# Threshold attention feeding a SoLU block: weights assembled by integer operations, early reciprocals on VectorE, one early block transfer on ScalarE's queue

## The chip, the cores and the metric

The kernel runs on one core of one Trainium2 chip. The metric is the device time of one execution in microseconds (us). All times here are in us unless marked otherwise. The engines are named as the profile names them: PE is TensorE (PEld its weight loads), DVE VectorE, ACT ScalarE, POOL GpSimd, SP SyncE; SPq and ACTq are the sequencers of SP and ACT while they issue a DMA.

## What is computed

Attention with a threshold on 8 batches of 8 heads, 576 tokens and 64 values a head, and then a feed-forward block over 4608 tokens:

```python
scores = scale * np.matmul(q, k.transpose(0, 1, 3, 2))
thresh = np.max(scores, axis=-1, keepdims=True) - tau
scores = np.where(scores >= thresh, scores, -1000000000.0)
scores = scores - np.max(scores, axis=-1, keepdims=True)
attn = np.exp(scores)
attn = attn / (np.sum(attn, axis=-1, keepdims=True) + 1e-09)
attn_out = np.matmul(attn, v)
...
x = attn_out.transpose(0, 2, 1, 3).reshape(B * S, H * D)
h = x @ w_in
solu = h * softmax(h)
ln = (solu - mean) / np.sqrt(var + 1e-06) * g_ln
return ln @ w_out
```

`q`, `k`, `v` are float32. `w_in` (512 x 1024) and `w_out` (1024 x 512) are float64; the launch hands them over as int64 words, and the kernel itself makes float32 of them from the two 32-bit halves.

## The kernel before, in words

The attention is cut into 144 *slots* of two heads by 128 rows of scores (18 a batch: kinds 0 and 1 are the 512 first columns of tokens, kind 2 the leftover 64). Two slots of the same heads are a *unit*. A Python loop walks over *rounds*, one new slot a round, and writes out by hand the order in which every engine gets its instructions; each engine then works through its own list in that order. In one round `rnd`:

- PE: `scores` (L480) of slot `rnd` into two PSUM tiles `s0`, `s1`. There is one buffer of each, so the next slot's scores wait until the ramps have read both.
- DVE: `maxes` (L502), for each of the two tiles the row extreme less the threshold, into `nth`.
- ACT: `ramp` (L517) of tile 0, then of tile 1, then `exps` (L526) of both, with the row sums into `sm`. Copies that prepare later heads (`keeps`, L382 to L427) stand between the two ramps in rounds with such items, and `whole_pair` copies after the exps in rounds 0, 2 and 4.
- POOL: `normalise` of slot `rnd - 1`: add 1e-9 (L533), power of -1 (L534), two products of the weights with the inverse (L536).
- DVE: `blocks` of slot `rnd - 1`: two transposes (L548) into `T`. After the second slot of a unit SP sends `T` to `wT` in three transfers (L557 for the middle partitions, L559 twice for the outer ones; kind 2 has four, L564).
- PE: `attend_steps` (L590), the product of `wT` with `v`, for a unit whose second slot is three rounds old (four in the first ones); ACT then copies it to `xh` (L622).
- PE: one of four steps of a feed-forward piece of 128 tokens: two h steps (L645, L655) and two o steps (L760), each half a piece's work, in successive rounds.

In rounds 0 to 15 one of 16 pieces of the weights (128 x 512 each; eight of `w_in` to `w1`, eight of `w_out` to `w2`) is made as well. `weight_load` (L275) brings the raw words, four rounds ahead. `weight_a` takes the exponent out of the high word on DVE (L286), turns it into a float scale on ACT (L291), and takes the mantissa bits (L292). `weight_b`, a round later, adds the low word (L306) and joins the sign to the scale (L309), both on DVE. `weight_c`, again a round later, multiplies the two on POOL (L319). For `w_out`, `weight_gain` first multiplies the scale by `g_ln` on ACT (L325), and `weight_d` sends the finished piece to its partner partitions on SP (L332, two transfers). `w2_done` is set with the last of these, in round 16; no o step is placed before that.

Two more facts of the order matter. POOL's `mark` (L109) waits for an h step of PE. Rounds past 16 in which no feed-forward step is under way are *loose*: there the maxima copy the scores out of PSUM, so that the ramps don't hold it.

## Time and profile before

| | |
|---|---|
| median of 3 runs | 866.67 us (865.36, 866.67, 873.14) |
| span of the profiled execution, first to last instruction | 865.3 us |
| instructions | 36120 |
| PE busy | 820.6 us, 95% |
| DVE busy | 682.6 us, 79% |
| ACT busy | 574.2 us, 66% |
| POOL busy | 500.2 us, 58% |
| DMA, queue of SP | 164.25 MB, 76.2% of 16 engines' span |
| DMA, queue of ACT | 2.00 MB, 0.7% |

The profiled execution has no time of its own in the list of runs; its span is what is known of it, and it lies 0.1 us under the fastest run. A busy share is a mean over the whole span: the first 100 us and the rest have different limits, so the prediction reads stretches of it. In the answers "x2" counts instructions, an arrow in brackets names what ended an idle time, and a line number is that of the kernel before.

### The profile page before, as it was taken

How to read it: one execution, taken by the hardware profiler on the slowest of the kernel's cores; microseconds unless marked ns; L12 is line 12 of the kernel's file. 1: busy time of each engine (PE TensorE's matmuls, PEld its weight loads, DVE VectorE, ACT ScalarE, POOL GpSimd, SP SyncE). 2: the span in 40 equal slices, each digit the busy share in tenths (PEclk: the TensorE clock that was granted, in tenths of full speed). 3: DMA queues.
4: the chain of work that ended last, by engine and by line, in shares of the span. 5: the costliest groups of instructions: out<-in, count | busy, mean ns of one | idle time of the engine just before them, and what ended most of it. 6: DMA issues, size and time to landing. Idle time of an engine off the chain costs nothing.

```text
span 865.3 us, 36120 instructions
## 1 busy us (share of the span) xinstructions
PE 820.6 (95%) x15361; PEld 633.6 (73%) x15361; DVE 682.6 (79%) x1248; ACT 574.2 (66%) x1153; POOL 500.2 (58%) x938
## 2 busy tenths in 40 slices
PE   5667999899999999999999999999999999999997
PEld 3444667677688887777777776777799998887655
DVE  4999778878788888888788887888888888787361
ACT  5887767767767767677677776777677776775121
POOL 2888656556656656565656655565666655555120
PEclk9788899999999999999999999999999999999999
DMA  8999787988878788988878877887788877655212
GB/s 256 273 261 238 192 190 176 229 237 203 222 188 232 200 191 197 225 221 191 212 190 223 204 188 186 220 221 203 190 224 229 205 180 189 154 142 139 69 38 62
DMA packets 83712, 168.54 MB, mean 195 GB/s; under 512 B 15448, under 2 KB 45152, under 8 KB 83552
## 3 DMA queue, kind: packets, MB, share of 16 engines
q1 hardware_dynamic: 82416, 164.25, 76.2%
q8 instruction: 120, 1.97, 1.0%
q10 hardware_dynamic: 1136, 2.00, 0.7%
q14 instruction: 40, 0.33, 0.1%
HBM read 46.14 MB, written 9.44 MB: 64 GB/s over the span
## 4 chain that ended last, share of the span: by engine, by line
PE 81%; DMA 7%; ACT 4%; DVE 2%; SPq 2%; issue 2%; POOL 1%; ACTq 0%; DVEq 0%
PE o_ps L760 26%; PE h_ps L655 22%; PE s_ps L480 15%; PE pv L590 15%; PE h_ps L645 3%; DMA wT<-T 3%; ACT w L517 1%; ACT w L526 1%; DMA ends<-in_q_dram 1%; DVE w L502 1%; DMA w<-w 1%; DMA qT<-flip 1%; DMA k<-in_k_dram 1%; DVE T L548 1%; POOL w L536 1%
## 5 line engine op out<-in xcount | busy, mean ns | idle before, releaser
L760 PE MATMUL o_ps<-w,uT 64*64 64x256 f32 x4608 | 274.3, 376 | 2.4 <-DMA w<-w 1.3
L502 DVE CUSTOM_DVE_ANT_0 w<-s_ps,tau_t 128x576 f32<-128x576 f32 x280 | 200.3, 753 | 87.5 <-PE s_ps L480 57.5
L517 ACT ACTIVATE w<-s_ps,nth 128x576 f32<-128x576 f32 x280 | 197.0, 739 | 104.9 <-DVE nth L502 94.1
L760 PEld LDWEIGHTS o_ps<-w,uT 64*64 64x64 f32 x4608 | 215.3, 133 | 62.8 <-ACT xh L622 11.0
L536 POOL TENSOR_SCALAR w<-w,sm 128x576 f32<-128x576 f32 x288 | 222.2, 784 | 14.3
L655 PE MATMUL h_ps<-w,xh 64*64 64x512 f32 x1856 | 225.3, 592 | 1.1 <-issue 1.1
L548 DVE STREAM_TRANSPOSE T<-w 128x576 f32<-128x576 f32 x288 | 207.6, 755 | 19.8 <-POOL w L536 19.4
L526 ACT ACTIVATE w<-w,ntau 128x576 f32<-128x576 f32 x288 | 219.6, 767 | 0.0
L590 PEld LDWEIGHTS pv<-wT,v 64*64 64x64 f32 x5760 | 179.0, 136 | 32.4 <-issue 8.5
L480 PE MATMUL s_ps<-kT,qT 64*64 64x64 f32 (+1 forms) x2048 | 183.2, 422 | 14.0 <-ACT w L517 12.1
L590 PE MATMUL pv<-wT,v 64*64 64x128 f32 (+1 forms) x5760 | 177.7, 264 | 7.4 <-DMA wT<-T 4.7
L655 PEld LDWEIGHTS h_ps<-w,xh 64*64 64x64 f32 x1856 | 134.8, 134 | 65.4 <-issue 15.6
L533 POOL TENSOR_SCALAR sm<-sm 128x2 f32<-128x2 f32 x144 | 36.5, 253 | 202.0 <-ACT w L526 198.9
L534 POOL TENSOR_TENSOR sm<-sm,mone 128x2 f32<-128x2 f32 x144 | 109.0, 757 | 12.0
L480 PEld LDWEIGHTS s_ps<-kT,qT 64*64 64x64 f32 x2048 | 78.3, 139 | 23.4 <-ACT w L517 17.3
L622 ACT COPY xh<-pv 128x256 f32<-128x256 f32 x64 | 25.2, 394 | 81.3 <-PE pv L590 81.3
L721 ACT ACTIVATE V<-u,nb,rs 128x1024 f32<-128x1024 f32 x36 | 44.7, 1241 | 38.8 <-POOL nb L711 31.8
L747 DVE STREAM_TRANSPOSE uT<-V 128x1024 f32<-128x1024 f32 x36 | 44.2, 1226 | 16.9 <-DMA V<-u 16.8
L526 ACT ACTIVATION_READ_ACCUMULATOR w<-w,ntau 128x1 f32 x288 | 55.5, 193 | 0.0
L685 DVE TENSOR_TENSOR u<-h_ps,u 128x1024 f32<-128x1024 f32 x36 | 42.8, 1189 | 9.8 <-ACT u L679 9.8
L726 DVE TENSOR_SCALAR u<-u,rs,nb 128x1024 f32<-128x1024 f32 x36 | 35.0, 973 | 17.8 <-ACT V L721 17.7
L670 DVE TENSOR_REDUCE hm<-h_ps 128x1 f32<-128x1024 f32 x36 | 42.9, 1193 | 5.4 <-PE h_ps L645 2.7
(90 smaller groups left out, 578.0 us busy)
## 6 DMA issues: line engine op xcount, KB each, us to landing
wT<-T SPq DMA_DIRECT2D x160, 288.0 KB, 6.3
wT<-T SPq DMA_DIRECT2D x64, 576.0 KB, 5.6
V<-u SPq DMA_DIRECT2D x144, 64.0 KB, 3.4
out_dram<-ob SPq DMA_DIRECT2D x71, 128.0 KB, 2.5
q<-in_q_dram SPq DMA_DIRECT2D x24, 288.0 KB, 6.2
qT<-flip SPq DMA_DIRECT2D x48, 144.0 KB, 3.5
k<-in_k_dram SPq DMA_DIRECT2D x24, 288.0 KB, 6.4
kT<-flip SPq DMA_DIRECT2D x48, 144.0 KB, 3.8
```

The lines of the kernel that those rows point to most:

```text
L480: nc.tensor.matmul(out=ps[h][ROWS[y], ks], lhsT=lhsT, rhs=d["kT"][ROWS[h], ks], start=True, stop=True,)
L502: nc.vector.tensor_tensor_reduce(out=w, in0=ps[:, 0:S], in1=(zero if loose else tau_t).to_broadcast([P, S]), scale=1.0, scalar=BIG, op0=AL ...
L517: nc.scalar.activation(out=d["w"][x], in_=d["w"][x] if d["loose"] else d["ps"][x][:, 0:S], func=AF.Prelu, bias=d["nth"][x], scale=-1.0, al ...
L526: nc.scalar.activation(out=w, in_=w, func=AF.Exp, bias=ntau, scale=1.0, accum_out=sm[:, x : x + 1])
L534: nc.gpsimd.tensor_tensor(out=sm, in0=sm, in1=mone, op=ALU.pow)
L536: nc.gpsimd.tensor_scalar(out=w, in0=w, scalar1=sm[:, x : x + 1], scalar2=1.0, op0=ALU.mult, op1=ALU.mult)
L548: nc.vector.transpose(out=T[:, :, r, h, :], in_=w)
L590: nc.tensor.matmul(out=to, lhsT=d["v"][ROWS[u], (h0 + h - u) % 4 if b > 1 else h0 + h, m ^ 4 * u if m < 8 and b < 2 else m,], rhs=rhs, sta ...
L655: mm = nc.tensor.matmul(out=h[ROWS[y], f], lhsT=x[ROWS[r], c, ROWS[y]], rhs=w1_parts[ROWS[r], c, part ^ r], start=part == 0 and c == 0, st ...
L721: nc.scalar.activation(out=V, in_=u, func=AF.Identity, bias=nb, scale=rs)
L747: nc.vector.transpose(out=uT, in_=d["V"].rearrange("p y (m x) -> p m y x", x=32))
L760: nc.tensor.matmul(out=d["o"][ROWS[z], 512 * (r ^ other) : 512 * (r ^ other) + 256], lhsT=d["uT"][ROWS[r], m].rearrange("p y x -> p (y x)" ...
```

## The change

- **Weights.** `weight_a` now masks the sign off the high word on DVE, makes a float-like word of the low one on ACT straight from the raw words (no longer from a result of DVE), and clamps the masked word on POOL. `weight_b` shifts that word by three bits and joins the sign, on DVE. `weight_c` adds the two words as integers on POOL, where it multiplied floats. What L306 did on DVE is gone. A unit of 0.5 remains, taken out by a scale in the copy to `xh` (L622, now an activation with a scale).
- **Gain.** `weight_gain` works on the finished piece, and so comes after `weight_c`: it and `weight_d` move from the round after a piece's round to the second after. `w2_done` is thereby set in round 17.
- **Reciprocals.** For slots below 20 the add and the power on POOL become an add and a reciprocal on DVE (`inverse`), at the end of the slot's own round, ahead of the next round's maxima in DVE's list.
- **Block transfer.** For slots below 24, the third transfer of a unit (the second of L559) is put off to the next round and issued on ACT's queue, after the first ramp.

On PE the order is the same up to slot 17. Then scores 18 follow scores 17 with no o step between, and the feed-forward steps run one step behind the old order until a later round that had none; the last 75 steps of PE stand in the same order. DVE has 21 entries more in its list, POOL 27 fewer, ACT 18 more, SP 11 fewer.

```diff
@@ -1,4 +1,5 @@
 from contextlib import ExitStack
+import struct
 import concourse.bass as bass
 import concourse.tile as tile
@@ -80,10 +81,11 @@
     scl = const.tile([P, 1], F32, name="scl")
     g_rows = work.tile([NC, P], F32, tag="V", bufs=1, name="g_rows")
     gs = const.tile([P, NC], F32, name="gs")
-    lims = [const.tile([P, 1], F32, name=f"lim{x}") for x in range(2)]
+    unit = const.tile([P, 1], F32, name="unit")
+    low = const.tile([P, 1], F32, name="low")
     wide = w_in.dtype == I64
-    W_UNIT = 2.0**-20 if wide else 1.0
+    W_UNIT = 0.5 if wide else 1.0
 
@@ -219,8 +221,8 @@
     def constants():
-        nc.gpsimd.memset(lims[0], 0.0)
-        nc.scalar.activation(out=ntau, in_=lims[0], func=AF.Exp)
+        nc.gpsimd.memset(zero, 0.0)
+        nc.scalar.activation(out=ntau, in_=zero, func=AF.Exp)
         make_identity(nc, ident)
         for g in range(2):
             of = 64 + 32 * (1 - g)
@@ -229,9 +231,7 @@
             )
         nc.gpsimd.memset(mhalf, -0.5)
         nc.gpsimd.memset(mone, -1.0)
-        nc.gpsimd.memset(zero, 0.0)
-        for l, e in zip(lims, (916, 896)):
-            nc.gpsimd.memset(l, -e * 8388608.0)
+        nc.gpsimd.memset(unit, 8388608.0)
 
@@ -259,12 +259,13 @@
         if x < 2 * NP:
             c, hf = divmod(x, 2)
             cols = slice(512 * hf, 512 * hf + 512)
-            return w_in[P * c : P * c + P, cols], w1[:, c, cols], W_UNIT
+            return w_in[P * c : P * c + P, cols], w1[:, c, cols], 1.0
         c = x - 2 * NP
         return w_out[P * c : P * c + P], w2[:, 2 * c], gs[:, c : c + 1]
     NW = 2 * NP + NC
     raws = {}
+    LEAST, MOST = [struct.unpack("f", struct.pack("I", x))[0] for x in (896 << 20, (1150 << 20) + 0xFFFFF)]
     def weight_load(x):
         raw = work.tile(
@@ -275,54 +276,56 @@
         queue.dma_start(out=raw, in_=piece(x)[0])
         raws[x] = dict(raw=raw)
+    def words(x):
+        both = raws[x]["raw"].bitcast(I32).rearrange("p (n two) -> p n two", two=2)
+        return both[:, :, 0], both[:, :, 1]
     def weight_a(x):
         if not wide:
             return
-        d = raws[x]
-        hi = d["raw"].bitcast(I32).rearrange("p (n two) -> p n two", two=2)[:, :, 1]
-        d["em"] = e, m = [
+        lo, hi = words(x)
+        raws[x]["em"] = r, m = [
             work.tile([P, 512], I32, tag=t, bufs=n, name="em") for t, n in (("ob", 2), ("xe", 1))
         ]
         nc.vector.tensor_scalar(
-            out=e, in0=hi, scalar1=20, scalar2=0x7FF,
-            op0=ALU.logical_shift_right, op1=ALU.bitwise_and,
-        )
-        nc.scalar.activation(out=e, in_=e, func=AF.Relu, bias=lims[x >= 2 * NP], scale=8388608.0)
-        nc.vector.tensor_scalar(
-            out=m, in0=hi, scalar1=0xFFFFF, scalar2=0x100000,
-            op0=ALU.bitwise_and, op1=ALU.bitwise_or,
+            out=m, in0=hi, scalar1=0x7FFFFFFF, scalar2=None, op0=ALU.bitwise_and
+        )
+        nc.scalar.activation(out=r, in_=lo.bitcast(U32), func=AF.Relu, bias=unit, scale=2.0**-29)
+        m = m.bitcast(F32)
+        nc.gpsimd.tensor_scalar(
+            out=m, in0=m, scalar1=LEAST, scalar2=MOST, op0=ALU.max, op1=ALU.min
         )
     def weight_b(x):
         d = raws[x]
-        _, dst, unit = piece(x)
+        _, dst, by = piece(x)
         if not wide:
-            nc.vector.tensor_scalar(out=dst, in0=d["raw"], scalar1=unit, scalar2=None, op0=ALU.mult)
+            nc.vector.tensor_scalar(out=dst, in0=d["raw"], scalar1=by, scalar2=None, op0=ALU.mult)
             return
-        words = d["raw"].bitcast(I32).rearrange("p (n two) -> p n two", two=2)
-        lo, hi = words[:, :, 0], words[:, :, 1]
-        e, m = d["em"]
+        _, hi = words(x)
+        m = d["em"][1]
+        nc.vector.tensor_scalar(
+            out=m, in0=m, scalar1=3, scalar2=0x3FFFFFFF,
+            op0=ALU.logical_shift_left, op1=ALU.bitwise_and,
+        )
         nc.vector.scalar_tensor_tensor(
-            out=dst, in0=lo.bitcast(U32), scalar=2.0**-32, in1=m, op0=ALU.mult, op1=ALU.add
-        )
-        nc.vector.scalar_tensor_tensor(
-            out=e, in0=hi, scalar=-(2**31), in1=e, op0=ALU.bitwise_and, op1=ALU.bitwise_or
+            out=dst.bitcast(I32), in0=hi, scalar=-(2**30), in1=m,
+            op0=ALU.bitwise_and, op1=ALU.bitwise_or,
         )
     def weight_c(x):
         d = raws.pop(x)
         if not wide:
             return
-        _, dst, _ = piece(x)
-        e, _ = d["em"]
-        nc.gpsimd.tensor_tensor(out=dst, in0=dst, in1=e.bitcast(F32), op=ALU.mult)
+        dst = piece(x)[1].bitcast(I32)
+        nc.gpsimd.tensor_tensor(out=dst, in0=dst, in1=d["em"][0], op=ALU.add)
 
     def weight_gain(x):
         if wide and x >= 2 * NP:
-            e = raws[x]["em"][0].bitcast(F32)
-            nc.scalar.activation(out=e, in_=e, func=AF.Copy, scale=piece(x)[2])
+            _, dst, by = piece(x)
+            nc.scalar.activation(out=dst, in_=dst, func=AF.Copy, scale=by)
 
     def weight_d(x):
@@ -527,15 +530,26 @@
                 out=w, in_=w, func=AF.Exp, bias=ntau, scale=1.0, accum_out=sm[:, x : x + 1]
             )
+    EARLY = NW + 4
+    def inverse(s):
+        sm = live[s]["sm"]
+        nc.vector.tensor_scalar(out=sm, in0=sm, scalar1=1e-9, scalar2=None, op0=ALU.add)
+        nc.vector.reciprocal(out=sm, in_=sm)
     def normalise(s):
         d = live[s]
         sm = d["sm"]
-        nc.gpsimd.tensor_scalar(out=sm, in0=sm, scalar1=1e-9, scalar2=None, op0=ALU.add)
-        nc.gpsimd.tensor_tensor(out=sm, in0=sm, in1=mone, op=ALU.pow)
+        if s >= EARLY:
+            nc.gpsimd.tensor_scalar(out=sm, in0=sm, scalar1=1e-9, scalar2=None, op0=ALU.add)
+            nc.gpsimd.tensor_tensor(out=sm, in0=sm, in1=mone, op=ALU.pow)
         for x, w in enumerate(d["w"]):
             nc.gpsimd.tensor_scalar(
                 out=w, in0=w, scalar1=sm[:, x : x + 1], scalar2=1.0, op0=ALU.mult, op1=ALU.mult
             )
+    BESIDE = 24
+    behind = []
     def blocks(s):
         b, kind, hp, r = slots[s]
@@ -555,8 +569,11 @@
         to = wT.rearrange("p g m r h x -> p g (m r h x)")
         if kind < 2:
             nc.sync.dma_start(out=to[:, 1], in_=T[32:96])
-            for half in range(2):
-                nc.sync.dma_start(out=to[ROWS[half], 0], in_=T[96 * half : 96 * half + 32])
+            nc.sync.dma_start(out=to[ROWS[0], 0], in_=T[0:32])
+            if s < BESIDE:
+                behind.append(lambda: nc.scalar.dma_start(out=to[ROWS[1], 0], in_=T[96:128]))
+            else:
+                nc.sync.dma_start(out=to[ROWS[1], 0], in_=T[96:128])
             return
         for g in range(2):
             for half in range(2):
@@ -619,7 +636,7 @@
                 )
             how = "p (r u y) -> p u r y" if b < 2 else "p (u g x r) -> p u g r x"
             to = xh[b, kind][:, hp].rearrange(how, u=2, r=2, **({} if b < 2 else {"g": 2}))
-        nc.scalar.copy(out=to, in_=y)
+        nc.scalar.activation(out=to, in_=y, func=AF.Copy, scale=W_UNIT)
         pairs_free.append(tag)
 
@@ -925,8 +942,8 @@
                     ready.pop(0)
             busy = cur is not None or prev is not None
             items = []
-            if rnd - 1 in pieces:
-                weight_gain(pieces[rnd - 1])
+            if rnd - 2 in pieces:
+                weight_gain(pieces[rnd - 2])
             if more:
                 room = SPARE
                 if busy and quarter > 1 and preps and rnd + 4 < first_slot(preps[0][3]):
@@ -948,6 +965,8 @@
                     keeps(rnd, 1)
                 maxes(rnd, loose)
                 ramp(rnd, 0)
+                while behind:
+                    behind.pop(0)()
                 if rnd == 0:
                     weight_a(0)
                 if not loose:
@@ -1048,11 +1067,13 @@
                         weight_load(y)
                 if x + 1 < len(pieces):
                     weight_a(x + 1)
+            if rnd < EARLY:
+                inverse(rnd)
             for job in load_at.pop(rnd, []):
                 job()
-            if rnd - 1 in pieces:
-                weight_d(pieces[rnd - 1])
-                w2_done = pieces[rnd - 1] == NW - 1
+            if rnd - 2 in pieces:
+                weight_d(pieces[rnd - 2])
+                w2_done = pieces[rnd - 2] == NW - 1
             rnd += 1
```

## The prediction, as it was put on record

> **What bounds the kernel now.** I read the page's slices first. TensorE (PE) is idle in tenths only in the first four or five slices of 21.6 us and in the tail; the change ends its special treatment at round 25, so only the start matters.
>
> ```profile
> PE   5667999899999999999999999999999999999997
> DVE  4999778878788888888788887888888888787361
> PEclk9788899999999999999999999999999999999999
> DMA  8999787988878788988878877887788877655212
> ```
>
> Then the busy time by stretches (us; PE, PEld, DVE, ACT, POOL, granted clock, DMA share, GB/s):
>
> ```profile
> 20.00:40.00 20.00, 13.96 (x267) 10.13 (x263) 19.53 (x42) 17.83 (x41) 16.89 (x20) 0.68 0.95 251
> 40.00:60.00 20.00, 13.01 (x240) 8.18 (x232) 19.81 (x42) 15.75 (x32) 16.61 (x20) 0.83 0.98 259
> 180.00:400.00 220.00, 218.94 (x4169) 172.12 (x4165) 184.26 (x335) 154.01 (x306) 135.51 (x263) 1.00 0.84 210
> ```
>
> From 20 to 60 us VectorE (DVE) is full (39.3 of 40) and PE two thirds busy; from 180 us PE is full. DMA is as full as DVE early, so a faster DVE meets it next. PE is idle some 37 us before 180; 10 of that is the first load. All gain must come from the other 27.
>
> One early round on DVE, in the timeline, then POOL's part of one:
>
> ```profile
> 34.46 1.05 DVE L306 SCALAR_TENSOR_TENSOR w<-raw,em 128x512 f32<-128x512 uint32 x1
> 35.44 0.68 DVE L309 SCALAR_TENSOR_TENSOR em<-raw,em 128x512 int32<-128x512 int32 x1
> 36.04 0.41 DVE L286 TENSOR_SCALAR em<-raw 128x512 int32<-128x512 int32 x1
> 38.07 1.43 DVE L548 STREAM_TRANSPOSE T<-w 128x576 f32<-128x576 f32 x2
> 39.42 0.77 DVE L306 SCALAR_TENSOR_TENSOR w<-raw,em 128x512 f32<-128x512 uint32 x1
> ...
> 40.52 0.65 POOL L533 TENSOR_SCALAR sm<-sm 128x2 f32<-128x2 f32 x1 [0.88 <-ACT w L526]
> 41.26 0.78 POOL L534 TENSOR_TENSOR sm<-sm,mone 128x2 f32<-128x2 f32 x1
> 42.14 1.48 POOL L536 TENSOR_SCALAR w<-w,sm 128x576 f32<-128x576 f32 x2
> 43.57 1.29 POOL L319 TENSOR_TENSOR w<-w,em 128x512 f32<-128x512 f32 x1
> ```
>
> L306 starts every 4.9 us: that is the round. Last, the chain that ended last, in order of time: it leaves DVE where `T` is sent to `wT` (the SP queue's two L559 issues take 2.8 us there), and PE then runs without a gap to 78 us.
>
> ```profile
> 55.67 6.69 DMA wT<-T
> 62.40 2.70 PE pv L590 x65
> ```
>
> **The change, part by part.**
>
> *Weights, DVE.* Counted start to start, L306 (0.65 to 0.98) goes; one shift/and replaces one and (0.33 each); the last bitwise step stays (0.61). A round was 2 x 0.68 maxima + 1.36 transposes + 0.8 + 0.61 + 2 x 0.33 = 4.8, with waits 4.9.
>
> *Reciprocal on DVE.* Two 128x2 operations are added; no row shows them in this place. Low: 0.08 each (the 128x1 accumulator read); high: 0.23 each (L509 on 128x2) and 0.1 of wait. I take 0.25 for both, near the plain small rows. POOL loses L533 and L534 (1.4 a round). New DVE round: 1.36 + 1.36 + 0.33 + 0.61 + 0.33 + 0.25 = 4.25; I use 4.35.
>
> *The wait it adds.* The inverse stands in DVE's queue ahead of the next maxima and waits for both exps of its round: first maximum 0.79, two ramps 1.31, two exps 1.62, 0.08, inverse 0.25 = 4.05 per round. That is below 4.35, so DVE still sets plain rounds. After rounds 2 and 4 ScalarE (ACT) copies a whole pair (1.65) and the weight activation (0.65) before the next ramp: 5.3, as now. Behind the inverse stand the maxima, behind those the ramps, PSUM and PE.
>
> *POOL.* New: a clamp on 128x512. Low 0.65 (L536 per element), high 1.29 (L319's size); I take 0.7, the same kind of operation as L536. The multiply becomes an integer add: low 0.65; high 3.8, since pow on 128x2 (0.72) against add (0.23) shows that an operation can cost three times another; I take 1.28, the same shape. Sum 0.7 + 1.47 + 1.28 = 3.45 in 4.35: hidden, and it stays hidden to an add of 2.2. Constants, the scale in the `xh` copy (at most 0.1 on an ACT that waits 81 us for pv there) and the weight activation's freedom from L286 cost nothing while ACT idles.
>
> *The block on ACT's queue.* Eleven units send their third transfer from ACT, after ramp 0 of the round after the one where SP would issue it. SP is spared 1.1 to 3.45 each. On ACT an issue that meets no backlog costs 0.45 to 0.72 (ACT's rows at 0.7 to 3 us), and ramp 0 covers 0.62; in a backlog it could hold ACT as SP is held. Low 0, high 3.45 - 0.62 = 2.8; I take 0, because ACT's queue carries nothing else then. What is surely lost is time: the block leaves later than `T` allows.
>
> The Trainium skill, page "DMA: Bandwidth & Descriptors", section "Issuing engines are not separate DMA queues", says that transfers from several issuing engines interleave on the same 16 DMA engines and that only sequencer time is saved. The trace's DMA share of 0.98 agrees that no bandwidth waits to be used; by that rule the second queue brings SP's time and no earlier landing.
>
> *Sum to 62 us.* With these rounds the ramp of round 9 starts at 53.4 (57.5 now), ramp 10 at 58.0 (62.2 now): 4.1 gained. But PE's full stretch starts on the third block of slots 6 and 7: issued at 55.67 now, at 53.5 then; with the median landing of 6.3 (L559: 6.5) it lands at 59.8 instead of 62.36: gain 2.5. If ACT's issue costs 0.6 uncovered: 54.9 + 6.3 = 61.2, gain 1.2. Taken: -2.5, ends -4.1 and 0.
>
> *62 to 105 us.* PE, and ACT after pv (xh, u, ramp 13), carry it; lengths unchanged: 0.
>
> *w2 one round later.* The gain and the copies move from the next round to the one after, for w2 as a whole (16 SP transfers of 128 KB, each past one more round's wT issues). The first o step needs the last piece. In the new order PE runs the scores of slots 17 and 18 with no o step between. Scores 18 need both ramps 17 (107.6 to 108.9 now) out of PSUM; PE, done with scores 17 at 106.4, has 2.6 us of nothing. The 1.3 us that the second o step waits for `w<-w` goes: +1.3. The later work is the same in amount, and the last 75 steps of PE stand in the same order.
>
> The gap may also chill PE. The trace has such gaps:
>
> ```profile
> 78.00:80.40 2.40, 0.02 (x2) 0.00 (x0) 2.40 (x7) 2.40 (x6) 1.75 (x3) 1.00 1.15 214
> 80.40:82.00 1.60, 1.24 (x32) 1.09 (x32) 1.60 (x3) 1.60 (x5) 1.43 (x3) 0.58 1.06 277
> 82.00:83.00 1.00, 0.54 (x20) 0.35 (x18) 1.00 (x2) 0.56 (x2) 0.48 (x2) 0.50 1.10 258
> ```
>
> After 2.4 us idle the clock fell to 0.5. An o step of 3.4 us at half clock costs up to 1.7 us for each 3.4 us cold. Low 0, high 3.4; I take 0.8, because the fall came later in some gaps and only part of the step would be cold. "TensorE: Matmul & The Clock Gate" (Part 1, HAM oscillation) advises against PE-idle gaps over about 3.4 us; by that rule a 2.6 us gap is harmless, the term is 0 and the sum 864.1; the row above, where 2.4 us sufficed, decides.
>
> **Sum.** -2.5 + 1.3 + 0.8 = -0.4. The profiled execution has a span of 865.3, 0.1 below the fastest run (865.36), so nothing to speak of lies around it; the median of the runs (866.67) is 1.4 above. 865.3 - 0.4 = 864.9.
>
> **Rivals.**
> *R1, the early gain arrives whole.* The third block is not what PE waits for, or lands faster, and no new cold gap appears: -4.1 + 1.3, and -4 more if the cold stretch of 82 to 94 us (h at 5.05 where 3.4 is warm, scores 2.2 where 1.2) goes: 858.5 to 862.5. For it: DVE's 19.8 of 20. Against: DMA share 0.98, which must then carry more per us.
> *R2, ACT is held by its DMA issue: slower.* Place: between ramp 0 and ramp 1 of rounds 3, 5, ... 15. SP's second L559 took 2.0, 1.1 and 3.45 there; less 0.62 of cover, 1.5 on average. Exps, inverse and maxima slip with it: odd rounds 4.05 + 1.5 = 5.6, beside even ones of 4.35 or 5.3, so two rounds take 9.95 or more against 9.9: the gain is gone, the block itself leaves later (+1.5), round 13 pays 1.5 on the chain, and w2 2.1: about 5, so 870. It decides from about 0.4 us held per issue, where it eats the -0.4.
> *R3, POOL's integer add is slow.* At 3.8 POOL needs 6.0 a round, 1.1 above the 4.9 of now; over the 10 rounds before PE is full 11, with w2 2: 878. For it only the pow row.
> *R4, nothing reaches PE.* DMA at 0.98 sets the early rounds anyway: gain 0, +1.3 to +3: 867.
>
> **How the numbers follow.** Forecast (own range 862 to 867) 0.45; R1 0.23; R4 0.12; R2 0.13; R3 0.07. Against the median of 866.67, faster by over 1% (about what a measurement of this kernel can tell from no change) is below 858.0: the fast end of R1, 0.10. Slower is above 875.3: most of R3 and the far end of R2, 0.08. The same: 0.82. The range 857 to 871 leaves out R3, the end of R2 and the extreme of R1.
>
> **What would show it.** Right: no L306; early rounds of about 4.35 on DVE; two small DVE operations right after exps; ACT's DMA row beside ramp 0 with ramp 1 not delayed; pv at about 60; a PE gap of 2 to 3 us before the first o step and no `w<-w` wait. Wrong: ramps 0 and 1 over 1 us apart in odd rounds (R2); the integer add over 2.2 (R3); pv still at 62 (R4); DVE rounds short and PE warm at 80 to 95 (R1).

## The result, and the profile after

The changed kernel takes 892.82 us (median of 4 runs, 891.89 to 895.47), the kernel before 866.01 on the same chip: ratio 1.0309, 95% interval 1.0265 to 1.0353. The forecast was 864.9, the range 857 to 871, and "slower" had 8 in 100: it was wrong. The profiled execution has a span of 890.1 us, 24.8 more than before's 865.3.

The slices of the page, the ones shown of before and POOL's:

```profile
PE   5667598988999999999999999999999999999997
DVE  4787886766788888888878887888878887777360
POOL 3777843635566666656566665656665665555120
PEclk9869699988999999999999999999999999999999
DMA  8888897768778877988788887888788877655312
```

As before, PE is short only at the start, but for longer: up to the tenth slice, 220 us. VectorE, which the forecast wanted a little shorter in its rounds, is now *less* busy there. The same two stretches as before (PE, PEld, DVE, ACT, POOL, granted clock, DMA share, GB/s) say it in numbers:

```profile
20.00:40.00 20.00, 11.98 (x197) 6.73 (x189) 15.86 (x37) 14.12 (x36) 14.49 (x13) 0.95 0.81 207
40.00:60.00 20.00, 13.06 (x192) 9.89 (x192) 15.83 (x38) 12.42 (x26) 13.99 (x13) 0.67 0.94 229
```

DVE fell from 39.3 to 31.7 of 40 us, the DMA share from 0.95 to 0.81 in the first stretch and from 0.98 to 0.94 in the second. No engine is full, and the DMA is less so than before. Where nothing is fuller and the round is still longer, work may be waiting in a ring: a chain of steps over several engines that closes on itself, so that its sum is the round. One round in the timeline of the changed kernel, DVE and POOL, some rows left out (start, duration, engine and line, the idle time before and what ended it):

```profile
21.64 0.43 DVE L290 TENSOR_SCALAR em<-raw 128x512 int32<-128x512 int32 x1
21.99 0.16 DVE L537 TENSOR_SCALAR sm<-sm 128x2 f32<-128x2 f32 x1
22.16 1.92 POOL L296 TENSOR_SCALAR em<-em 128x512 f32<-128x512 f32 x1 [1.57 <-DVE sm L537]
22.18 0.17 DVE L538 RECIPROCAL sm<-sm 128x2 f32<-128x2 f32 x1
...
24.18 1.46 POOL L547 TENSOR_SCALAR w<-w,sm 128x576 f32<-128x576 f32 x2
24.95 1.50 DVE L562 STREAM_TRANSPOSE T<-w 128x576 f32<-128x576 f32 x2 [1.26 <-POOL w L547]
25.61 1.29 POOL L322 TENSOR_TENSOR w<-w,em 128x512 int32<-128x512 int32 x1
26.38 0.80 DVE L308 TENSOR_SCALAR em<-em 128x512 int32<-128x512 int32 x1
27.21 0.69 DVE L312 SCALAR_TENSOR_TENSOR w<-raw,em 128x512 int32<-128x512 int32 x1
27.93 0.43 DVE L290 TENSOR_SCALAR em<-raw 128x512 int32<-128x512 int32 x1
28.46 1.92 POOL L296 TENSOR_SCALAR em<-em 128x512 f32<-128x512 f32 x1 [1.56 <-DVE sm L537]
```

The clamp starts at 22.16 and again at 28.46: the round is 6.29 us, where it was 4.9. Both engines have a gap in it, POOL 1.57 (it waits for DVE's masked word), DVE 1.26 (it waits for POOL's weights). The row of the clamp names L537, the inverse's add, since that was the last to end before it, at 22.15; the mask L290 had ended at 22.07. In the version below that has no such add (the integer weights alone) the same gap of 1.57 is put down to L290. The ring can be read off: clamp 1.92, hand-over 0.10, normalising 1.43, integer add 1.29, the end of the shift 0.28 later, 0.03, join 0.69, 0.03, mask 0.43, hand-over 0.10: 6.30. All three of POOL's steps lie in it, one after the other.

The second loss shows in PE's waits, between 150 and 220 us, and in the order of SP's queue ahead of it:

```profile
PE pv L607 <- DMA v<-in_v_dram: 5.8, 1, 5.8
```
```profile
169.81 3.48 SPq L754 DMA_DIRECT2D V<-u  x4
173.33 2.06 SPq L812 DMA_DIRECT2D out_dram<-ob  x2
175.65 1.22 SPq L217 DMA_DIRECT2D qT<-flip  x2
176.91 1.31 SPq L179 DMA_DIRECT2D v<-in_v_dram  x2
178.27 1.27 SPq L184 DMA_DIRECT2D v<-in_v_dram  x2
```

PE waits 5.8 us for values that left SP behind a feed-forward piece's exchange and store; in the kernel before the same load left at 159.24, ahead of that exchange, and pv waited 0.7.

A ruler for both: the start of a slot's first exp, changed kernel less kernel before.

| slot | 4 | 8 | 12 | 18 | 24 | 26 | 27 | 32 | 48 | 128 |
|---|---|---|---|---|---|---|---|---|---|---|
| later by, us | 3.3 | 8.7 | 13.5 | 13.4 | 16.6 | 15.1 | 25.0 | 21.3 | 26.2 | 24.2 |

It loses 1.3 us a round from slot 4 to slot 12, nothing to slot 18, and then again from slot 18 on, 10 of it between slots 26 and 27.

### The profile page after: what moved, and what is told of

Same layout as the page of the kernel before. It is cut to its first block, busy times and chain, and to the rows that moved or that the text cites. A ratio compares the mean times of both kernels' runs of the same rounds, so it can differ in the third digit from the quotient of the medians.

```text
span 890.1 us, 36136 instructions
## 1 busy us (share of the span) xinstructions
PE 829.5 (93%) x15361; PEld 642.4 (72%) x15361; DVE 681.6 (77%) x1270; ACT 575.5 (65%) x1153; POOL 505.0 (57%) x912
## 4 chain that ended last, share of the span: by engine, by line
PE 81%; DVE 5%; DMA 5%; POOL 3%; SPq 2%; issue 2%; ACT 1%; ACTq 0%; DVEq 0%
PE o_ps L777 26%; PE h_ps L672 21%; PE s_ps L483 15%; PE pv L607 14%; PE h_ps L662 3%; DMA wT<-T 3%; POOL em L296 2%; DMA v<-in_v_dram 2%; DVE T L562 2%; POOL w L547 1%; DVE w L505 1%; DVE w L312 1%; DVE em L308 1%; PE s_ps L348 1%; SPq L754 1%
## 5 line engine op out<-in xcount | busy, mean ns | idle before, releaser
L520 ACT ACTIVATE w<-s_ps,nth 128x576 f32<-128x576 f32 x284 | 200.2, 739 | 119.4 <-DVE nth L505 105.5
L777 PEld LDWEIGHTS o_ps<-w,uT 64*64 64x64 f32 x4608 | 230.3, 134 | 47.4 <-ACT xh L639 11.0
L672 PE MATMUL h_ps<-w,xh 64*64 64x512 f32 x1856 | 221.7, 589 | 1.2 <-POOL mark L111 1.2
L483 PE MATMUL s_ps<-kT,qT 64*64 64x512 f32 (+1 forms) x2048 | 184.5, 429 | 23.5 <-ACT w L520 21.0
L607 PE MATMUL pv<-wT,v 64*64 64x128 f32 (+1 forms) x5760 | 180.4, 268 | 14.7 <-DMA wT<-T 6.2
L672 PEld LDWEIGHTS h_ps<-w,xh 64*64 64x64 f32 x1856 | 127.6, 133 | 70.6 <-issue 25.1
L544 POOL TENSOR_SCALAR sm<-sm 128x2 f32<-128x2 f32 x124 | 28.8, 232 | 172.9 <-ACT w L529 169.9
L545 POOL TENSOR_TENSOR sm<-sm,mone 128x2 f32<-128x2 f32 x124 | 92.3, 744 | 10.3
L639 ACT ACTIVATE xh<-pv 128x256 f32<-128x256 f32 x64 | 25.7, 402 | 87.7 <-PE pv L607 87.7
L296 POOL TENSOR_SCALAR em<-em 128x512 f32<-128x512 f32 x16 | 30.7, 1921 | 32.7 <-DVE sm L537 22.5
```

The source lines that it names most:

```text
L296: nc.gpsimd.tensor_scalar(out=m, in0=m, scalar1=LEAST, scalar2=MOST, op0=ALU.max, op1=ALU.min)
L483: nc.tensor.matmul(out=ps[h][ROWS[y], ks], lhsT=lhsT, rhs=d["kT"][ROWS[h], ks], start=True, stop=True,)
L520: nc.scalar.activation(out=d["w"][x], in_=d["w"][x] if d["loose"] else d["ps"][x][:, 0:S], func=AF.Prelu, bias=d["nth"][x], scale=-1.0, al ...
L545: nc.gpsimd.tensor_tensor(out=sm, in0=sm, in1=mone, op=ALU.pow)
L607: nc.tensor.matmul(out=to, lhsT=d["v"][ROWS[u], (h0 + h - u) % 4 if b > 1 else h0 + h, m ^ 4 * u if m < 8 and b < 2 else m,], rhs=rhs, sta ...
L672: mm = nc.tensor.matmul(out=h[ROWS[y], f], lhsT=x[ROWS[r], c, ROWS[y]], rhs=w1_parts[ROWS[r], c, part ^ r], start=part == 0 and c == 0, st ...
```

## The experiments

Two theories go with these readings. *Loop*: POOL's clamp is dear and stands in a serial ring, about 14 us. *Second weights*: their last steps a round later cost 9 to 11 us. Rivals: the integer add on POOL, POOL's sheer load, or the placing of other parts. The kernel before was timed beside each.

| run | ratio to before, 95% interval | median, us |
|---|---|---|
| changed kernel | 1.0309 (1.0265 to 1.0353) | 892.82 |
| clamp as two products | 1.0179 (1.0149 to 1.0209) | 881.28 |
| clamp twice | 1.0653 (1.0624 to 1.0683) | 921.85 |
| before, second weights late | 1.0127 (1.0090 to 1.0163) | 877.06 |
| after, second weights early | 1.0208 (1.0177 to 1.0239) | 883.49 |
| no clamp, second weights early | 1.0037 (1.0010 to 1.0064) | 869.33 |
| before, inverse on DVE | 0.9985 (0.9955 to 1.0014) | 866.64 |
| before, third block on ACT | 1.0027 (0.9997 to 1.0057) | 869.41 |
| integer weights alone | 1.0322 (1.0272 to 1.0372) | 895.27 |
| values' load a round earlier | 1.0293 (1.0242 to 1.0344) | 892.07 |
| clamp behind the normalising | 1.0379 (1.0329 to 1.0429) | 899.02 |
| the same without the add | 1.0270 (1.0228 to 1.0312) | 888.16 |
| clamp on DVE, second weights early | 1.0055 (1.0020 to 1.0089) | 872.61 |
| no clamp, half the weight loads | 1.0016 (0.9988 to 1.0045) | 867.63 |
| second weights first in their round | 1.0233 (1.0207 to 1.0259) | 884.34 |

### The price of the clamp

```diff
         nc.gpsimd.tensor_scalar(
-            out=m, in0=m, scalar1=LEAST, scalar2=MOST, op0=ALU.max, op1=ALU.min
+            out=m, in0=m, scalar1=1.0, scalar2=1.0, op0=ALU.mult, op1=ALU.mult
         )
```

> The changed kernel with the clamp's two operations (maximum, minimum) replaced by two multiplications by 1.0 on the same tile and engine, so that nothing is clamped. Theory L (the clamp's length stands in a loop from DVE over POOL back to DVE, and maximum and minimum are slow on POOL): the instruction falls from 1.92 to about 0.7 us, the early round from 6.29 to about 5.1, some 15 us go by slot 16, the time is about 877. Rival I (the inverse's wait for the exps sets the round): the round stays 6.29 and the time 892. Rival P (any instruction of this form takes 1.9 there because DVE shares the port): 1.9 and 892.

The timeline of POOL with two products, one round:

```profile
35.69 0.62 POOL L296 TENSOR_SCALAR em<-em 128x512 f32<-128x512 f32 x1 [1.56 <-DVE sm L537]
36.28 1.47 POOL L547 TENSOR_SCALAR w<-w,sm 128x576 f32<-128x576 f32 x2
37.71 1.28 POOL L322 TENSOR_TENSOR w<-w,em 128x512 int32<-128x512 int32 x1
```

Same tile, same engine, same instruction form, two other operations: 0.62 instead of 1.92. The round is 4.87 (the next of these starts at 40.56), slot 10 is only 0.4 us late, and 11.5 us of the loss are gone. The forecast's 0.7 was right for a product and wrong for max and min.

The clamp done twice (the same instruction again) is the other direction:

> The changed kernel with the clamp issued twice in a row. Theory L (serial loop): every early round grows by the whole 1.95, to about 8.2, and 13 to 16 such rounds add 25 to 31 us: about 920. Rival O (POOL's occupancy counts, not the order): POOL has 4.7 us of work in a round of 6.3, so 1.6 of the second clamp is free and the rounds grow by 0.3: about 897. Rival I (inverse and exps): no change, 892.

The transposition, in DVE's timeline of this version, now waits 3.27 us for POOL's weights where it waited 1.26:

```profile
31.60 1.50 DVE L565 STREAM_TRANSPOSE T<-w 128x576 f32<-128x576 f32 x2 [3.27 <-POOL w L550]
...
39.88 1.50 DVE L565 STREAM_TRANSPOSE T<-w 128x576 f32<-128x576 f32 x2 [3.27 <-POOL w L550]
```

The round is 8.28: 1.99 more, the whole of the second clamp. The time rose by 29.0 us over the changed kernel, 16 times 1.92 are 30.7. So nothing hides any part of it; a POOL with 1.57 us to spare in each round would have hidden most if spare time were what counts.

### The second weights, put late and put early

In the kernel before, only the round of `weight_d` and of `w2_done` changes:

```diff
-            if rnd - 1 in pieces:
-                weight_d(pieces[rnd - 1])
-                w2_done = pieces[rnd - 1] == NW - 1
+            if rnd - 2 in pieces:
+                weight_d(pieces[rnd - 2])
+                w2_done = pieces[rnd - 2] == NW - 1
```

> The kernel before with one thing changed: the copies of the finished w2 pieces and the mark that all are there come one round later, so that PE and SP get the changed kernel's order of feed-forward steps. Theory W (this order puts the V and output transfers ahead of the second half of v in SP's list, and PE waits for v near slot 26; and it opens a gap before the first o step): 4 to 10 us slower, 870 to 876, with a wait of pv for v of several us. Rival (the order is harmless by itself, v was late because the early rounds were long): within 2 us of before.

11 us slower (by the ratio), with 6.0 us of waiting for the values where before waited 0.7:

```profile
PE pv L590 <- DMA v<-in_v_dram: 6.0, 1, 6.0
```

The reverse in the changed kernel (the gain right behind `weight_c`, `weight_d` and `w2_done` for piece `rnd - 1`):

> The changed kernel with the gain on the finished piece right behind its integer add in the same round, and copies and mark in the kernel before's round, so that PE's and SP's order of feed-forward steps is the old one. Theory W: the wait for v near slot 26 (9 us between slots 26 and 27) and the gap before the first o step go, 881 to 884; the early rounds keep 6.29. Rival (the order is harmless): 892.

883.49: 9 us of the loss are gone, pv waits 0.5 for the values, the rounds stay at 6.28. Slot 12 is 13.6 us late as in the changed kernel, slot 128 15.3 instead of 24.2.

### Both away

```diff
-        m = m.bitcast(F32)
-        nc.gpsimd.tensor_scalar(
-            out=m, in0=m, scalar1=LEAST, scalar2=MOST, op0=ALU.max, op1=ALU.min
-        )
```

with the second weights early as above.

> The changed kernel with two things away: the clamp on GpSimd (max and min) is left out, so the weights are not bounded before the shift, and the second weights' last steps come one round after the load's arithmetic, as in the kernel before. Theory L+W (the clamp makes the early rounds 6.29 us long, and the second weights a round late push the values' load behind the feed-forward's exchange on SyncE's queue; nothing else of the change costs over 3 us): 862 to 868, rounds 4.9 us or less. Rival (a third part of the change costs as well, such as the VectorE shift beside GpSimd, the inverse on VectorE or the block transfer on ScalarE's queue): over 870.

869.33, ratio 1.0037: nearly all of the 3.1% was these two. From the ratios, against 866 us: clamp 1.0208 to 1.0037, 15 us; second weights 1.0309 to 1.0208, 9 us; 3 us left (0.9 to 5.5). The 1.33 us above the expected band is small beside that, but the gain that the forecast looked for is not there either. DVE's round is indeed shorter, 4.66 (its shift starts at 37.20 and 41.86), and slot 8 is 2.8 us early, yet at slot 12 it is 1.2 us late: pv waits 7.0 us for block transfers between 50 and 80 us, before 1.9.

```profile
DMA  9999999999999999999999999998998997999999
...
wT<-T SPq DMA_DIRECT2D x3, 288.0 KB, 11.8
```

Those lines are the DMA view of that version from 40 to 75 us, the share in 40 slices and the median of a transfer from issue to landing: no slice is under 9 until 63 us, and a block takes 11.8 us; in before's profile 5.9. To see whether that is the limit, every second piece of weights is not loaded (the arithmetic is done on the piece before it):

```diff
     def weight_load(x):
+        if x % 2:
+            raws[x] = dict(raw=raws[x - 1]["raw"])
+            return
```

> The version without the clamp and with the second weights early, and each second piece of weights is not loaded (the arithmetic is done on the piece before it): 8 of 16 transfers of 512 KB are left out. Theory D (with the clamp away the early rounds are bound by the DMA engines: the share is 1.02, a block's transfer lands in 11 us instead of 6, and pv waits 7.0 us for blocks between 50 and 80 us where it waited 1.9 before): the waits for blocks fall below 2.5 us, the landing below 8 us, and the time to 860 to 865. Rival (VectorE or TensorE's clock sets the early rounds there too): 867 to 871.

Not settled. Landing fell to 6.7 to 8.0, the waits for blocks to 3.9, and slot 18 was 3.4 us early; but 2.2 us of that went between slots 18 and 20, and the rest by slot 24, a stretch in which PE stood 3.00 us after the fifteenth product of an o step. The rows name no releaser for that wait; the last section finds one.

```profile
132.57 1.13 PE L777 MATMUL o_ps<-w,uT 64*64 64x256 f32 x15
136.70 3.02 PE L777 MATMUL o_ps<-w,uT 64*64 64x256 f32 x49 [3.00 <-issue]
```

867.63 is above the band of the theory and within the rival's. Also, the next two versions have rounds as long as before and still show landings of 8.6 to 10.5, so the landing is not a pure effect of shorter rounds; before's 5.9, from its one profile, may be a good draw. What is shown: an early gain of 3 us did not reach the end.

### The other parts alone

The inverse on DVE, in the kernel before:

```diff
+    def inverse(s):
+        sm = live[s]["sm"]
+        nc.vector.tensor_scalar(out=sm, in0=sm, scalar1=1e-9, scalar2=None, op0=ALU.add)
+        nc.vector.reciprocal(out=sm, in_=sm)
...
+            if rnd < EARLY:
+                inverse(rnd)
```

> The kernel before with one part of the change: the early rounds' sums of exponentials are inverted on VectorE. It takes about 0.9 us off GpSimd's part of a round and puts 0.27 us on VectorE, which is full in the early rounds of before. Theory 1 (VectorE sets the early round of before): slower by up to 20 x 0.27 = 5 us, 866 to 871. Theory 2 (the round of before is set by the loop over GpSimd and the block transfers): faster by up to 5 us, 860 to 865.

Neither: 0.9985, no difference. Rounds of 5.01 us on DVE (L306 at 33.74 and 38.75) and POOL's load cut from 16.9 to 10.9 of 20 us: what was taken off POOL was idle time there, what was put on DVE is 0.1 us a round.

The third block transfer on ACT's queue, in the kernel before:

```diff
-            for half in range(2):
-                nc.sync.dma_start(out=to[ROWS[half], 0], in_=T[96 * half : 96 * half + 32])
+            nc.sync.dma_start(out=to[ROWS[0], 0], in_=T[0:32])
+            if s < BESIDE:
+                behind.append(lambda: nc.scalar.dma_start(out=to[ROWS[1], 0], in_=T[96:128]))
+            else:
+                nc.sync.dma_start(out=to[ROWS[1], 0], in_=T[96:128])
```

> The kernel before with one part of the change: the third of a unit's block transfers is issued from ScalarE's queue in the first 24 rounds. Theory 1 (the issue of 0.55 us lies behind the first ramp in slack): 864 to 867. Theory 2 (the transfer lands a SyncE issue earlier and pv is brought forward): 860 to 864. Rival (ScalarE is held behind the issue until the transposition is through): 868 to 875.

1.0027 (0.9997 to 1.0057): nothing, or a trifle slower. The issue takes 0.55 us and begins with ramp 0, which covers it:

```profile
37.04 0.74 ACT L517 ACTIVATE w<-s_ps,nth 128x576 f32<-128x576 f32 x1
37.04 0.55 ACTq L563 DMA_DIRECT2D wT<-T  x1
37.71 0.74 ACT L517 ACTIVATE w<-s_ps,nth 128x576 f32<-128x576 f32 x1
```

The integer weights alone (the changed kernel with `EARLY = 0`, `BESIDE = 0` and the second weights early):

> The changed kernel with the integer weights alone: the inverse stays on GpSimd, all block transfers on SyncE's queue, and the second weights' last steps one round after the arithmetic, as in the kernel before. The clamp of 1.92 us and the GpSimd inverse of about 0.9 us then lie in one queue. Theory S (the early round is the serial loop clamp, inverse, normalise, transposition, shift, join): rounds of 6.9 to 7.3 us and about 890 to 900. Rival (the inverse is hidden beside other work): rounds of 6.3 us, 881 to 885.

The serial ring again: POOL's inverse (0.24 and 0.71, with gaps 1.1 us) now lies in it too, and the clamp starts at 30.72 and 38.14, a round of 7.42:

```profile
30.72 1.93 POOL L296 TENSOR_SCALAR em<-em 128x512 f32<-128x512 f32 x1 [1.57 <-DVE em L290]
32.73 0.24 POOL L544 TENSOR_SCALAR sm<-sm 128x2 f32<-128x2 f32 x1
33.05 0.71 POOL L545 TENSOR_TENSOR sm<-sm,mone 128x2 f32<-128x2 f32 x1
```

So the same early inverse on DVE that is worth nothing in the kernel before is worth 1.1 us a round beside the clamp, some 10 us in all (1.0322 against 1.0208; the two versions also differ in the third block's queue, which alone made no clear difference). A part's worth belongs to the ring it stands in.

### Where in the ring

The clamp behind the normalising in POOL's queue; every instruction is the same (the clamp moves out of `weight_a` into a function `clamp`):

```diff
                 normalise(rnd - 1)
+            if wide and rnd in pieces:
+                clamp(pieces[rnd])
```

> The changed kernel with the clamp behind the normalising in GpSimd's queue; all instructions are the same. Theory S (the early round is a serial chain over VectorE and GpSimd, so the place of the 1.92 us in the queue counts): normalising no longer stands behind the clamp, the clamp runs beside the transposition, rounds of 5.6 to 5.9 us instead of 6.29, and 882 to 886. Rival (what counts is GpSimd's occupancy, 4.7 us of work plus what it waits): rounds stay at 6.2 or more and the time at 891 to 894.

A clear miss: 899.02, rounds of 6.66, and the reason is in one row of POOL's timeline beside one of DVE's:

```profile
33.64 1.28 POOL L324 TENSOR_TENSOR w<-w,em 128x512 int32<-128x512 int32 x1
...
33.70 1.49 DVE L310 TENSOR_SCALAR em<-em 128x512 int32<-128x512 int32 x1 [0.96 <-POOL em L298]
```

The shift takes 1.49 us here, 0.80 in the changed kernel, 0.39 in places. Wherever it is longer than 0.43, in every version, it ends 0.27 to 0.32 us after POOL's add: 35.19 against 34.92 here, 27.18 against 26.90 in the changed kernel, 37.78 against 37.49 without the clamp (shift 0.58). It isn't slow, it is held until the add is through. To test that, the add is left out of this version (the low words are not added):

> The version with the clamp behind the normalising, and GpSimd's integer add of the low words left out (the weights lose their last bits). Theory K (VectorE's shift can't run while GpSimd's two-input add runs: in every version it ends 0.26 to 0.29 us after the add does, 0.39 us long where it starts later, 1.49 us where it starts with it): the shift falls from 1.49 to 0.4 us, rounds from 6.66 to 5.5 to 5.7 us, and the time from 899 to 882 to 886. Rival (the shift is slow because it reads what GpSimd has just written, or by its operands): the shift stays at 1.4 to 1.5 us, rounds at 6.5 us or more, 896 to 900.

```profile
37.00 0.43 DVE L310 TENSOR_SCALAR em<-em 128x512 int32<-128x512 int32 x1 [1.00 <-POOL em L298]
37.46 0.69 DVE L314 SCALAR_TENSOR_TENSOR w<-raw,em 128x512 int32<-128x512 int32 x1
```

The shift is 0.43, still right behind the clamp that it waits for, and the round 5.58 (31.42 to 37.00): the hold is the add's, not the operands'. The time of 888.16 is 2 us above the band, within its interval. The Trainium skill, page "SBUF — State Buffer", section "SBUF: two separate sides", says that VectorE and GpSimd share a pair of SBUF ports under an exclusive lock: a GpSimd operation, and a VectorE operation in a two-port mode or with two SBUF inputs, shut each other out, and the one that comes second stands until the other is over. These rows agree, with 0.27 us from the add's end to the shift's; in which mode the shift runs, no row shows. DVE's transposes take 1.43 us both in this version, which has no add, and without the clamp, where the add runs beside them: they show no such hold.

The kernel before has the same hold, in the multiply (L319) that stood where the add stands now:

```profile
33.69 1.28 POOL L319 TENSOR_TENSOR w<-w,em 128x512 f32<-128x512 f32 x1
38.37 1.28 POOL L319 TENSOR_TENSOR w<-w,em 128x512 f32<-128x512 f32 x1
```

They end at 34.97 and 39.65, and the two L306 rows that the prediction shows (1.05 us from 34.46, 0.77 from 39.42) end at 35.51 and 40.19, 0.54 later both times. So it is in all ten rounds in which the two overlap (0.54 to 0.56); where the multiply is over, L306 takes 0.65 to 0.69. So 0.1 to 0.4 us a round of the busy time that made DVE look full was standing.

### Whose order: the values' load and the planner

If the 9 us of the second weights are the values' load behind the exchange in SP's queue, putting that load a round earlier takes them away:

```diff
-        (PER + 7, load_v, 1, (1, 2)),
+        (PER + 6, load_v, 1, (1, 2)),
```

> The changed kernel with one load moved: the second and third parts of the values' load for the second batch's second half are issued one round earlier, which puts them ahead of the feed-forward's exchange on SyncE's queue. The second weights stay one round late. Theory Q (the 9 to 10 us at slot 27 are that load standing in queue order behind the exchange): the wait of 5.8 us of pv for v goes, 880 to 884. Rival (each feed-forward step is a round later and the wait is only where the loss shows): still 889 or more.

A miss: 892.07. PE's wait for the values fell as wanted:

```profile
PE pv L607 <- DMA v<-in_v_dram: 1.9, 1, 1.9
```

But slot 27 is still 21.9 us late and slot 128 22.5 (24.2 without the edit). PE waits for other things in the new order (3.7 for blocks, 2.3 for something that the rows do not name). Between slots 16, 18, 20, 24, 27, 32 and 48 the granted clock is 0.86, 0.97, 0.93, 0.92, 1.00 and 0.96; with the second weights early it is 1.00 in all but one of these stretches (0.94). So the values' wait is where the loss shows, not what it is.

The last run leaves the weights' steps a round late but puts them first in that round, so that the planner sees `w2_done` in time and starts the o steps in the same round as before:

```diff
             if rnd - 2 in pieces:
                 weight_gain(pieces[rnd - 2])
+                weight_d(pieces[rnd - 2])
+                w2_done = pieces[rnd - 2] == NW - 1
```

> The changed kernel with the second weights' swap transfer (and the note that they are done) at the head of its round, right behind the gain, instead of at its end: the data come less than a round earlier, but the planner starts the feed-forward's second product in the round in which it started it before the change. Theory P (the 9 us of the second weights are the planner's: every feed-forward step moves by a round and meets other loads, waits and a colder TensorE): TensorE waits for the weights for 3 to 6 us once, no wait of 5 us for the values at slot 27, and 883 to 888. Rival (the lateness of the data costs it): 889 to 893.

```profile
PE o_ps L777 <- DMA w<-w: 1.8, 1, 1.8
```

884.34. PE waits 1.8 us for the weights, less than I expected, there is no wait for values, and slot 27 is 15.9 late, as with the weights early. (That profile is of the fastest of the five runs, 877.98; the others took 881.57 to 885.66.) By the ratios some 6.6 of the 9 us (with intervals of 2 to 4 us) go with the planner's order: one flag set after the round instead of before it, and every feed-forward step moves by a round. The transfer moved forward with the flag, by less than a round, so this run does not part the two wholly. What the moved order loses piece by piece (waits, clock) I have shown only in part.

## Why the prediction was wrong, point by point

The step that failed is POOL's part of the early round: a clamp taken at 0.7 us, and a sum of 3.45 us taken as hidden in a round of 4.35. The runs showed a clamp of 1.92 us in a ring over DVE and POOL that made the round 6.29, some 15 us of the 27 lost. The second step that failed is the sum's term for the second weights: 2.1 us where they cost 9.

- **"POOL ... a clamp on 128x512 ... I take 0.7, the same kind of operation as L536".** Failed. Max and min took 1.92, a product 0.62. The high end, 1.29, was too low as well: the row that warned (pow on 128x2 three times an add) was used to bound the integer add alone, which then took 1.28, exactly as taken. It was the other operation that cost three times.
- **"Sum 0.7 + 1.47 + 1.28 = 3.45 in 4.35: hidden".** Failed in kind, not only in size. With the true clamp the sum is 4.67, and the round became 6.29, not 4.7. The text added up one engine's work and set it against the other's round. But the change had tied them: mask (DVE), clamp (POOL), normalising and add behind it in POOL's queue, shift and join (DVE), next mask. The forecast's question for "hidden" should have been whether the chain from a mask to the next mask fits, waits included. The clamp twice (rounds of 8.28) and the integer weights alone (7.42) show the ring.
- **"one shift/and replaces one and (0.33 each)".** Failed: start to start the shift took 0.83, as it is held until POOL's add ends. The rows of before showed such a hold: L306 of 1.05 and 0.77 us, each ending 0.54 us after POOL's multiply. The forecast took its spread of 0.65 to 0.98 as a price and did not ask what made it.
- **"New DVE round ... I use 4.35".** Without the clamp it was 4.66: start to start the shift took 0.61 instead of 0.33 (it is held there too), the join 0.73 instead of 0.61. Even then the early gain was not kept.
- **"w2 one round later ... +1.3. The later work is the same in amount, and the last 75 steps of PE stand in the same order".** Failed in size: 9 (changed kernel) to 11 us (kernel before) where the sum had 2.1 with the cold clock. The near part came as told: a gap of 1.85 us before scores 18 (2.6 was estimated), and the o step behind it at 5.08 us (3.8 when warm). What was missed is that all steps of a stretch of the order move against loads whose round is fixed. The same amount of work is no argument when its neighbours change.
- **The inverse on DVE, 0.25.** Right: 0.27 start to start (0.19 and 0.08), and in the kernel before the move changes nothing.
- **The block on ACT's queue, 0, "no earlier landing".** Right: issues of 0.54 to 0.58 beside ramp 0, one hold of 2.65 in round 13, and the part alone at 1.0027 (at most 5 us by its interval).
- **The rivals.** R2 (ACT held) and R3 (a slow integer add) fell. R3 had the right engine and the wrong instruction. R1's whole early gain did not come even without the clamp. R4, nothing reaches PE, is about what the change makes without its two losses: 867 forecast, 869.33 measured.
- **The range.** It ended at 871; the one rival with a slow POOL operation (R3: 3.8 us, 878) had 7 in 100 and was left out of it. Two new kinds of operation on POOL, neither with a row, deserved that chance each, and in the ring even 1.92 us alone made 883 (the version with the second weights early).
- **"865.3, 0.1 below the fastest run ..., so nothing to speak of lies around it".** Misread. In every run on record the time is 1.7 to 2.1 us longer than the span, so a span of 865.3 belongs to a time near 867, and the sum should have stood on that. It makes the forecast 2 us too fast, which is small beside the rest.

## What to carry to other kernels

When a change hands a tile from one engine to another and back within a round, write down the ring (each step's length, the hand-overs, what stands ahead in each queue) and compare its sum with the round; two engines with idle time on both sides can still be slower. Price an operation by a row of the same operation, not of the same shape, and where there is none let the high end be several times the nearest row. A flag that a planner reads is a lever on everything planned behind it: set it in the round in which it was set, even if the work behind it must wait a little.

The clamp can be had almost for nothing on DVE. The version below computes all that the changed kernel does, with the second weights early:

```diff
-        nc.gpsimd.tensor_scalar(
+        nc.vector.tensor_scalar(
             out=m, in0=m, scalar1=LEAST, scalar2=MOST, op0=ALU.max, op1=ALU.min
         )
```

> The changed kernel with the clamp on VectorE and the second weights' last steps one round after the arithmetic: all that the change computes, with both causes away. One float max and min of 128x512 is taken at 0.41 us by VectorE's other operations on that tile, on top of the 4.66 us round of the version without a clamp. Theory: rounds of 5.0 to 5.1 us, as before the change, and 866 to 872. Rival (max and min are as dear on VectorE as on GpSimd, 1.9 us): rounds of 6.5 us and over 885.

DVE's timeline of this version:

```profile
35.21 0.43 DVE L290 TENSOR_SCALAR em<-raw 128x512 int32<-128x512 int32 x1
35.67 0.43 DVE L296 TENSOR_SCALAR em<-em 128x512 f32<-128x512 f32 x1
```

The clamp takes 0.43 us on DVE, the round is 5.13, and the time 872.61, ratio 1.0055 (1.0020 to 1.0089): some 22 us better than the changed kernel, by the ratios. No version beat the kernel before by more than its interval.

## What the runs showed of the hardware that was not expected

- On GpSimd, max and min by two constants on a 128x512 float32 tile take 1.92 us, two products 0.62, an integer add of two such tiles 1.28. On VectorE the same max and min take 0.43.
- A VectorE shift of 0.39 to 0.43 us on such a tile can't run beside GpSimd's integer add: it ends 0.27 to 0.32 us after the add, and takes 0.58, 0.80 or 1.49 us by when it began. The two-input L306 of the kernel before ends 0.54 to 0.56 us after GpSimd's multiply in the same way. VectorE's transposes are not held.
- TensorE stood 0.8 to 3.0 us after the fifteenth product of one o step in seven versions (the changed kernel is not among them), and 0.5 at most in an o step of the kernel before; the rows name no releaser. The DMA records do. Queue q8, "instruction" on the page, brings 120 packets of 16 KB, one for about every 256 of PE's entries (15361 products, as many weight loads, and some others). In all 16 traces, from the ninth packet on, an entry of PE at one and the same place in every 256 never starts earlier than 1.2 us after a packet has ended, and each of these seven waits ends at such an entry, 1.3 to 1.6 us after the packet (for the 3.00 us shown above the packet ran from 134.08 to 135.18 and the product began at 136.70). The unnamed waits of pv with the second weights late (2.4 in the kernel before, 2.3 with the values' load moved, 1.0 in the changed kernel) end the same way. So, as far as the records show, TensorE waits there for its own instructions, fetched late. It happens with the second weights early (2.25) as well as late, so it does not explain what they cost; no run here was made to vary it.
